# Small transfers of a recurrence loop on ScalarE's hardware DMA queue instead of GpSimd's software queue

## The chip, the cores and the metric

One core of one Trainium2 chip. The metric is the device time of one execution in microseconds, lower is better. Engines are named as in the profile: PE (matmul), PEld (its weight load), DVE (VectorE), ACT (ScalarE), POOL (GpSimd), SP (SyncE); a `q` behind a name is that engine's instruction queue, which issues DMA transfers. L658 is a line of the kernel's source.

## The reference, cut to what matters

There are two independent parts. Part A is a long convolution and is the first 440 us of the kernel; the change does not touch it. Part B is a recurrence over 64 segments of 32 tokens with 8 tokens of memory:

```python
mem = mem0                                              # [1, 8, 1024]
for s in range(64):
    h = concat([mem, x[:, 32*s:32*s+32]], axis=1)       # 40 tokens
    q, k, v = (einsum('btd,dhe->bhte', h, W) for W in (Wq, Wk, Wv))   # 32 heads of 128
    o = attention(q, k, v)                              # memory tokens are seen by all
    o = einsum('bhte,hed->btd', o, Wo)
    mem = o[:, :8]                                      # goes into the next step
    outs.append(o[:, 8:])                               # 32 tokens to the output
```

Every step needs all four weight matrices (64 chunks of 512 KB), and step s+1 can't start before `mem` of step s is there.

## The kernel before

Most weight chunks stay in SBUF. Those that don't fit, 19 in each step, are streamed from a scratch tensor `WS` into a ring of six slots by SP. A chunk is fetched as soon as PE has used up the one whose slot it takes:

```python
RING = 6
def slot():
    k = free.pop(0)
    t = ring.tile([128, 2048], BF, tag=f"wring{k}", name="wring")
    return k, t
def fetch():
    if loads:
        s, ch = loads.pop(0)
        live[s, ch] = k, t = slot()
        nc.sync.dma_start(t[:], stream_src(ch))      # 512 KB
def done(ch):                                        # behind the matmuls of a streamed chunk
    free.append(live.pop((now[0], ch))[0])
    ...
    fetch()
```

The small transfers of a step, all from GpSimd, in software:

```python
def load_x(s):                        # 192 KB: the tokens and last tokens' K and Q of step s
    rec = one.tile([128, 768], BF, tag="rec", name="rec")
    nc.gpsimd.dma_start(rec[:], REC[:, s, :])
    ...
class Tail:                           # output rows of two steps together, every second step
    def store(self):
        YB = one.tile([128, 256], BF, tag="QT", name="YB")
        nc.vector.tensor_copy(YB[:], self.acc)
        for dq in range(4):           # 4 x 8 KB
            nc.gpsimd.dma_start(bass.AP(outb.tensor, ..., [[2048 * SEG, NB], [2048, 8], [1, 256]]),
                                YB[32 * dq:32 * dq + W, :])
# ... in each step s
VBs = one.tile([128, 2, 128], BF, tag="VBs", name="VBs")       # 64 KB: last tokens' V
nc.gpsimd.dma_start(VBs[:]..., VBD[s].rearrange("t c i w -> (c i) t w"))
# ... projections, attention, output projection
if not last: load_x(s + 1)            # behind the last V projection
# ...
nc.scalar.copy(Y[:], yacc[:, 0:256])
nc.gpsimd.dma_start(bass.AP(outb.tensor, outb.offset + SEG * s * 2048,
                            [[256, 4], [2048, 32], [1, 256]]), Y[:])   # 64 KB, rows of 512 bytes
```

One thing is not in the source: the build. It gives each hardware transfer, whether from SP or from ACT, one of eight completion semaphores, in turn and in the order of the program. A transfer that gets a semaphore waits at its issue until the last transfer that had it has landed. Before, the chunks of 600 to 2100 us use eight semaphore numbers, each 133 times. I call this order of hardware transfers "the row" below. Software transfers have eight semaphores of their own (before, numbers 111 to 118).

## Time and profile before

| | |
|---|---|
| median of 3 runs | 2195.88 us (2193.15 to 2203.36) |
| profiled span | 2198.0 us, granted TensorE clock 0.965 |
| first Y copy / last Y copy in the trace | 496.7 us / 2185.4 us |
| one step, mean | 26.80 us |

The prediction below shows the views that it rests on. How to read them: in the DMA view a queue's share is the time that its packets took, as a share of 16 engines' time; q1 is SP's hardware queue, q10 ACT's, q0 the software queue. In the waits of SP's queue, `SPq L658 <- X: total, times, longest` says how long the issue of a weight chunk stood still and what ended the wait last. The moved bytes of the loop, 600 to 2100 us:

```profile
DMA packets 166936, 581.58 MB, mean 388 GB/s; under 512 B 25758, under 2 KB 25758, under 8 KB 166648
```

### The profile page before, as it was taken

The page shows a single profiled execution, that of the slowest core. Times are in us where ns is not written, and L with a number is a line of the kernel's source. Part 1 is how long each engine was busy: PE and PEld are TensorE (multiplying, and loading weights), DVE is VectorE, ACT ScalarE, POOL GpSimd, SP SyncE. Part 2 cuts the span into 40 slices and gives each one's busy share as a digit, 9 for nine tenths or more (in the row PEclk, how much of TensorE's full clock was granted, in tenths as well). Part 3 has the DMA queues.
Part 4 walks back from the last instruction along what each step waited for, and adds up shares of the span by engine and source line. Part 5 has one row for each costly group of instructions (what it writes and reads, how often), then busy time and mean ns, then how long its engine had stood idle before and what let it go on. Part 6 is the DMA issues. An engine that isn't in the chain of part 4 may idle for free. (4 is left out here: it accounts for less than half of the span.)

```text
span 2198.0 us, 81500 instructions
## 1 busy us (share of the span) xinstructions
PE 1721.9 (78%) x35607; PEld 927.7 (42%) x35636; DVE 884.2 (40%) x2702; ACT 638.6 (29%) x1118; POOL 412.2 (19%) x1103
## 2 busy tenths in 40 slices
PE   4679975957777788878888888887887878888886
PEld 2233332424444444444444444444444444444444
DVE  8827853123333333333333333333333333333332
ACT  5845530112222222222222222222222222222222
POOL 5004331001111112111111111111111211211111
PEclk9889997879999999999999999999999999999999
DMA  9989989899999999999999999999999999999997
GB/s 322 345 291 342 318 238 325 275 346 390 386 380 378 381 374 390 385 378 395 391 392 395 391 393 393 392 397 365 396 392 387 394 390 376 388 392 388 390 385 273
DMA packets 294286, 807.80 MB, mean 368 GB/s; under 512 B 84940, under 2 KB 84972, under 8 KB 293927
## 3 DMA queue, kind: packets, MB, share of 16 engines
q1 hardware_dynamic: 263592, 738.36, 89.0%
q0 software_dynamic: 23536, 50.51, 6.8%
q10 hardware_dynamic: 6800, 13.72, 1.7%
q8 instruction: 279, 4.57, 0.9%
q14 instruction: 79, 0.65, 0.1%
HBM read 743.06 MB, written 62.39 MB: 366 GB/s over the span
## 5 line engine op out<-in xcount | busy, mean ns | idle before, releaser
L806 PEld LDWEIGHTS <-rec 128*32 128x32 bf16 x12351 | 324.2, 96 | 471.6 <-issue 255.0
L806 PE MATMUL acc<-wring,rec 128*32 128x512 bf16 (+1 forms) x3777 | 374.7, 385 | 136.0 <-DMA wring<-WS 122.1
L815 ACT CAST qkv_sb<-acc 128x512 bf16<-128x512 f32 x384 | 224.8, 585 | 676.2 <-PE acc L806 645.7
L806 PE MATMUL acc<-Wres,rec 128*32 128x512 bf16 x4864 | 394.9, 383 | 1.5 <-issue 1.4
L892 PEld LDWEIGHTS <-OT 128*32 128x32 bf16 x8192 | 217.8, 96 | 178.1 <-issue 151.6
L892 PE MATMUL yacc<-Wlate,OT 128*32 128x256 bf16 x5120 | 221.8, 274 | 13.0 <-issue 11.9
L892 PE MATMUL yacc<-wring,OT 128*32 128x256 bf16 x3072 | 153.9, 276 | 98.5 <-DMA wring<-WS 59.0
L806 PE MATMUL acc<-Wmid,rec 128*32 128x512 bf16 x3072 | 226.1, 383 | 0.5 <-issue 0.5
L752 PEld LDWEIGHTS <-OTB 128*16 128x16 bf16 x4096 | 104.5, 89 | 103.9 <-issue 94.0
L878 ACT CAST OT<-OTp 128x512 bf16<-128x512 f32 x128 | 74.9, 585 | 241.4 <-PE OTp L870 241.3
L707 POOL DMA_DIRECT2D rec<-REC x64 | 37.4, 584 | 566.6 <-issue 268.9
L908 DVE COPY KT<-tps 128x512 bf16<-128x512 bf16 x64 | 27.2, 424 | 289.1 <-PE tps L821 289.1
L879 DVE CAST OTB<-OTp 128x128 bf16<-128x128 f32 x128 | 37.3, 291 | 258.6 <-ACT OT L878 258.6
L647 DVE TENSOR_SCALAR wring<-OTp 128x384 int32<-128x384 int32 x126 | 112.2, 890 | 61.5 <-PE acc L806 54.2
L752 PE MATMUL SB<-Wlate,OTB 128*16 128x256 bf16 x2480 | 98.0, 277 | 35.4 <-DVE SB L743 19.3
L782 POOL COPY KT<-rec 128x128 bf16<-128x128 bf16 x128 | 38.6, 302 | 439.2 <-PE SB L830 430.9
L836 DVE TENSOR_REDUCE mx<-SB 128x5 f32<-128x200 f32 x128 | 47.1, 368 | 182.8 <-PE SB L830 182.8
L767 POOL DMA_DIRECT2D out_dram<-YB x128 | 73.1, 578 | 236.4 <-DVE YB L765 212.9
L752 PE MATMUL SB<-wring,OTB 128*16 128x256 bf16 x1488 | 78.8, 274 | 36.5 <-DVE SB L731 30.8
L821 PE MATMUL tps<-ident,qkv_sb 128*128 128x128 bf16 x1024 | 101.2, 221 | 7.8 <-DVE wring L647 0.2
L821 PEld LDWEIGHTS <-qkv_sb 128*128 128x128 bf16 x1024 | 62.7, 97 | 104.7 <-ACT qkv_sb L815 64.4
L556 PE MATMUL kb_ps<-XBT,pw 128*128 128x512 bf16 x314 | 87.7, 400 | 9.3 <-ACT XBT L512 7.6
(214 smaller groups left out, 2300.8 us busy)
## 6 DMA issues: line engine op xcount, KB each, us to landing
wring<-WS SPq DMA_DIRECT2D x1218, 512.0 KB, 7.3
rec<-REC POOLq DMA_DIRECT2D x64, 192.0 KB, 6.0
SK<-s_sb SPq DMA_DIRECT2D x16, 512.0 KB, 4.8
SU<-s_sb SPq DMA_DIRECT2D x16, 512.0 KB, 4.6
Ug<-SU SPq DMA_DIRECT2D x32, 256.0 KB, 6.1
Kg<-SK ACTq DMA_DIRECT2D x32, 256.0 KB, 5.5
REC<-stage SPq DMA_DIRECT2D x4, 2048.0 KB, 15.2
SZ<-zs SPq DMA_DIRECT2D x31, 256.0 KB, 3.0
```

Of the source, the lines that this page charges most:

```text
L556: nc.tensor.matmul(ps[:], lhsT=ws[kc][:, hl * 128:(hl + 1) * 128], rhs=XBT[:, kc].rearrange("p s t -> p (s t)"), start=(kc == 0), stop=(kc ...
L647: nc.vector.tensor_scalar(out=dst, in0=src, scalar1=0, scalar2=None, op0=ALU.bitwise_or)
L707: nc.gpsimd.dma_start(rec[:], REC[:, s, :])
L752: nc.tensor.matmul(self.acc[32 * dq:32 * dq + W, x - o:y - o], lhsT=self.OTB[:, c, 4 * g + i, :], rhs=r, start=first and not self.seeded, ...
L767: nc.gpsimd.dma_start(bass.AP(outb.tensor, outb.offset + (SEG * NB * self.b + NX) * 2048 + 256 * dq, [[2048 * SEG, NB], [2048, 8], [1, 256 ...
L782: nc.gpsimd.tensor_copy(KT[:, :, :, 32:40], KBs[:, 128 * g:128 * g + 128].rearrange("p (c i t) -> p i c t", c=4, i=4))
L806: nc.tensor.matmul(self.acc[32 * c:32 * c + 32, x - 512 * c:y - 512 * c], lhsT=hT[:, kc, :], rhs=r, start=(kc == 0 and x == 512 * c), stop ...
L815: nc.scalar.copy(sb[:], self.acc[:])
L821: nc.tensor.transpose(tp[:, i * 128:(i + 1) * 128], sb[:, i * 128:(i + 1) * 128], ident[:])
L836: nc.vector.tensor_reduce(out=mx[:], in_=S, op=ALU.max, axis=AX.X)
L878: nc.scalar.copy(OT[:], o_view[:, :, :, 0:32])
L892: nc.tensor.matmul(yacc[32 * dq:32 * dq + 32, x - o:y - o], lhsT=OT[:, c, i, :], rhs=r, start=(h == 0 and x == o), stop=(h == 31), tile_po ...
```

## The change

The intent: in the kernel before, GpSimd's software queue costs 0.55 to 0.7 us of GpSimd for each issue and shows the first data packet some 4 us after it (3.8 us for the YB stores, median of 600 to 2100 us); I expected ACT's hardware queue to be quicker. The core of the diff (in its other lines YB's copy and YB's stores become two methods, `copy()` and `store()`, so that the stores follow the Y store):

```diff
     def load_x(s):
         rec = one.tile([128, 768], BF, tag="rec", name="rec")
-        nc.gpsimd.dma_start(rec[:], REC[:, s, :])
+        (nc.gpsimd if s == 0 else nc.scalar).dma_start(rec[:], REC[:, s, :])
@@ Tail.store
                 for dq in range(4):
-                    nc.gpsimd.dma_start(
+                    nc.scalar.dma_start(
@@ each step
-            nc.gpsimd.dma_start(VBs[:].rearrange("p g e -> p (g e)"), VBD[s].rearrange("t c i w -> (c i) t w"))
+            nc.scalar.dma_start(VBs[:].rearrange("p g e -> p (g e)"), VBD[s].rearrange("t c i w -> (c i) t w"))
@@
+            V1 = pv1.evac()
             if not last:
                 load_x(s + 1)
-            V1 = pv1.evac()
@@
-            nc.gpsimd.dma_start(bass.AP(outb.tensor, outb.offset + SEG * s * 2048, [[256, 4], [2048, 32], [1, 256]]), Y[:])
+            nc.scalar.dma_start(bass.AP(outb.tensor, outb.offset + SEG * s * 2048, [[256, 4], [2048, 32], [1, 256]]), Y[:])
             if tail is not None and not last:
                 tail.run(TURN[1])
+            if finished is not None:
+                finished.store()
```

More of the change, by code (lines that the diff above doesn't have):

```diff
@@ L741, in __init__ @@
                 self.seeded = acc is None
+                self.YB = None
                 self.left = list(range(32))
@@ L756, in head @@
                 if not self.left:
-                    self.store()
+                    self.copy()
             def run(self, n):
@@ L761, in run, with copy @@
                     self.head(h, pieces((3, h // 2, 0)))
+            def copy(self):
+                self.YB = one.tile([128, 256], BF, tag="QT", name="YB")
+                nc.vector.tensor_copy(self.YB[:], self.acc)
             def store(self):
-                YB = one.tile([128, 256], BF, tag="QT", name="YB")
-                nc.vector.tensor_copy(YB[:], self.acc)
+                YB, self.YB = self.YB, None
+                if YB is None:
+                    return
                 for dq in range(4):
-                    nc.gpsimd.dma_start(
+                    nc.scalar.dma_start(
                         bass.AP(outb.tensor, outb.offset + (SEG * NB * self.b + NX) * 2048 + 256 * dq,
@@ L948, in b_kernel @@
             nc.scalar.copy(Y[:], yacc[:, 0:256])
+            finished = tail
             if j == NB - 1 and not last:
@@ L954, in b_kernel @@
                 fill_mem(pend[s + 1][0], Y)
-            nc.gpsimd.dma_start(bass.AP(outb.tensor, outb.offset + SEG * s * 2048, [[256, 4], [2048, 32], [1, 256]]), Y[:])
+            nc.scalar.dma_start(bass.AP(outb.tensor, outb.offset + SEG * s * 2048, [[256, 4], [2048, 32], [1, 256]]), Y[:])
             if tail is not None and not last:
                 tail.run(TURN[1])
+            if finished is not None:
+                finished.store()
             if last:
                 own.run(32)
+                own.store()
 @with_exitstack
```

## The prediction

The sum came to +97 us over 2195.9: 81 for the 31 steps with YB stores, 21 for the 33 others (0.65 us each, "engine load"), and about -5 for the end; that made 2293, and less 8 for rival 2 it is the 2285. The 21 us rested on which DMA engines take a store's rows from step to step, and the records, which do not name the engine of a packet, don't show that. The sum of rival 3 and the ground for the 2330 of rival 4 rested on the same.

> **What bounds the kernel now.** I read first the busy strip of the page, then the chain of work that ended last, then the DMA view of the middle of the loop, then the waits of SP's queue, and last the timeline of one step's end.
>
> The strip has one digit (tenths busy) for each of 40 slices of 55 us:
>
> ```profile
> PE   4679975957777788878888888887887878888886
> ...
> DMA  9989989899999999999999999999999999999997
> ```
>
> From slice 9 on (the recurrence, 64 steps from about 460 us to the end) PE is 80% busy and the 16 DMA engines are never free. The chain, followed back through the last 380 us or so, agrees: of the 17% of the span that it covers, 11 are weight chunks on their way into the ring.
>
> ```profile
> DMA 11%; PE 3%; DVE 2%; issue 1%; ACT 0%; POOL 0%; SPq 0%; DVEq 0%; POOLq 0%; ACTq 0%
> ```
>
> The DMA view of 600 to 2100 us (queue: packets, MB, share of the engines' time; then issues with KB and us to landing) holds 56 steps, so a step is 1500/56 = 26.8 us:
>
> ```profile
> q1 hardware_dynamic: 153208, 557.89, 96.2%
> q0 software_dynamic: 13440, 19.42, 3.9%
> ...
> wring<-WS SPq DMA_DIRECT2D x1064, 512.0 KB, 7.2
> rec<-REC POOLq DMA_DIRECT2D x56, 192.0 KB, 6.1
> out_dram<-Y POOLq DMA_DIRECT2D x56, 64.0 KB, 6.4
> VBs<-VBD POOLq DMA_DIRECT2D x56, 64.0 KB, 6.3
> out_dram<-YB POOLq DMA_DIRECT2D x112, 8.0 KB, 5.0
> ```
>
> A step has 19 chunks of 512 KB (1064/56), one each 1.35 us; all the small transfers together take 3.9%, 1.04 us. A chunk lands 7.2 us after its issue, so 7.2/1.35 = 5.3 of the six ring slots are on their way: the queue is full, and this depth is what keeps the engines busy. What makes SP wait (us in total, times, longest):
>
> ```profile
> SPq L658 <- PE acc L806: 461.1, 681, 3.7
> ...
> SPq L658 <- DMA wring<-WS: 282.4, 559, 2.0
> ```
>
> SP issues a chunk as soon as a slot is free. So only two things can move the time: what the busiest DMA engine has to do in a step, and whether SP can keep the queue filled.
>
> [...] in 440 to 480 us the hardware queue of ACT,
>
> ```profile
> q10 hardware_dynamic: 1568, 3.16, 23.2%
> ```
>
> holds in the packet records 1440 data packets and 128 completions: 16 for each of six weight loads and 8 for each of the four loads of 8 rows. [...] In the records, packets of the record load do stand alternately with chunk packets. [...] the YB stores issued at 1381.46 us show their first data packet at 1385.4.
>
> **The change part by part.**
>
> Issue cost. GpSimd loses 0.55 to 0.7 us for each of its transfers; it is not in the chain, so nothing comes of it but at the end. ACT gains them. Its old hardware issues took about 0.33 us (256 KB loads). One step's end:
>
> ```profile
> 1380.96 0.37 ACT L948 CAST Y<-yacc 128x256 bf16<-128x256 f32 x1 [3.39 <-PE yacc L892]
> ...
> 1381.46 2.29 POOL L767 DMA_DIRECT2D out_dram<-YB  x4 [6.59 <-DVE YB L765]
> ...
> 1383.74 0.69 POOL L955 DMA_DIRECT2D out_dram<-Y  x1
> ...
> 1384.42 0.55 POOL L778 DMA_DIRECT2D VBs<-VBD  x1
> ...
> 1386.70 0.58 ACT L815 CAST qkv_sb<-acc 128x512 bf16<-128x512 f32 x1 [5.37 <-PE acc L806]
> ```
>
> ACT is idle for 5.4 us just there; six issues of 0.33 are 2 us. The record load after the V evacuation falls into another gap. Cost on the path: 0.
>
> Engine load. In the records a software packet joins descriptors to 4096 bytes (159 to 170 ns, as a chunk's packet), but a hardware packet is one row. A 512-byte row: between 464 and 467 us ten rows and ten completions,
>
> ```profile
> q10 hardware_dynamic: 20, 0.01, 0.8%
> ```
>
> are 0.8% of 48 engine-us, 0.38 us; less ten completions of 9 ns, 29 ns a row. (The records say 27.) [...]
>
> Queue depth, the part that I hold to be the largest. The build gives every hardware transfer one of eight completion semaphores in turn, and a transfer waits for the last user of its own. In the kernel before only chunks stand in that row, and 8 back is never behind the six slots. Now Y, four YB and VBs stand in it too. The listing of SP's instructions with their waits, at the end of a step with YB stores (the wait after the comma is the slot's own):
>
> ```
> 544 L658 DMACopy wring_13350<-WS_59 128x2048 [waits DMAHW7_49,DMAHW2_49,PE_49]
> 545 L658 DMACopy wring_13378<-WS_59 128x2048 [waits DMAHW4_49,DMAHW0_49,PE_49]
> 546 L658 DMACopy wring_13446<-WS_59 128x2048 [waits DMAHW5_49,DMAHW1_49,PE_49]
> ```
>
> HW4 is the Y store's, HW5 the first YB store's. So chunk 13378 can't be issued before Y has landed, and SP keeps order, so nor can any later one. In the trace before it was issued at 1380.73, before Y was even copied. Worked out on those times: the chunks on their way at 1380.7 (issued at 1374.84, 1376.34, 1379.74, and the next, held until about 1382) last for 4 x 1.35 = 5.4 us, to about 1386.1. Y is issued at 1381.4 and starts at about 1383 (my estimate); to 1386.1 16 of its 32 rows pass, each in turn with a chunk packet (27 + 162 ns); the rest need 16 x 27 = 0.4 us and the landing some 0.5: Y lands at about 1387, the next chunk's data come 1.7 us later (estimate), 1388.7. The engines stand for 1388.7 - 1386.1 = 2.6 us. YB's rows and half of Y's pass in that hole, so the engine load of such a step is mostly inside it. A step without YB has three semaphores fewer in the way: there Y's is due seven chunks on, when Y has landed or nearly so; no hole.
>
> Sum: 31 steps with YB x 2.6 = 81; [...] the end of the kernel, where GpSimd's eight stores of 0.57 us stand in the chain, about -4 or -5. Together +97, so about 2293; I take some of it back for rival 2: **2285 us**.
>
> **The rivals.**
> 1. Nothing but the issuer changes: the DMA time is the same, and the software queue's 4 us to the first packet were hidden. For it: small transfers are 3.9%. Against it: the waits above, which are in the program. It would make 2190 to 2200.
> 2. The software queue disturbs the chunks, and its going helps. In the records a chunk packet within 0.2 us of a software packet takes 175.8 ns on average, one far from any 164.9; that is up to 0.35 us a step, 22 us in all. Alone it would make about 2170; with the rest it softens the rise.
> 3. Only the engine load counts, the semaphore waits are met early[...].
> 4. QT0 waits for the landing of YB (same buffer). [...] Then 2330 or more.
>
> **Range and chances.** Rival 3 and a hole of 1.5 us set the low side, 2215; rival 4 or a hole of 4 us the high side, 2350. Within 2% ends at 2240: that needs the hole to be nearly absent or the engine load to be spread. Slower by over 2% 0.86, within 0.12, faster by over 2% 0.02.
>
> **What would show it.** Right: in the waits of SP's queue, new rows of chunks waiting for out_dram<-Y or <-YB with one to several us each in some 31 steps; the strip of DMA falls below 9 in slices, and GB/s of the loop from 388 to about 368; the share of a software queue in the loop is 0, q10 has 128 + 128 + 128 row packets a step and more; steps with YB longer than the others by 2 us. Wrong: the DMA share stays at 100% with the time up (engine load or slower packets, not depth), or ACT waits for DMA ahead of an evacuation that PE needs, or the time stays and the waits for Y are short because a hardware store lands much sooner than I estimate.

What the traces show beside its figures:

- Engines. In the packet records a hardware transfer sends 16 completion packets, or fewer; I take one as one engine's. After, in 600 to 2100 us, the counts fit 16 for the record, 16 for VBs, 4 for Y and 2 for each YB store (53 x 36 + 26 x 8 = 2116, all there are). So Y is 32 rows on each of four engines.
- Packets. Before, software packets have 4096 bytes (median 165 ns, the middle half 159 to 174), those of the record 4608 and 3072; a chunk's packets have 4096 (median 162 ns, 159 to 165). After, a row of 512 bytes is one packet, median 27 ns.
- Alternation. Before, the last two packets of the record load issued at 1374.30 start 0.342 us apart, which is the 180 ns of the first and one chunk packet (162). After, the last rows of Y in the step of 1394.8 pass 0.18 us apart.
- Its estimates of 1.6 us from Y's issue to its first row, 0.5 to the landing and 1.7 from a chunk's issue to its data give no source. Before, the ACT load issued at 128.72, after 116 us without a packet on its queue, took 1.56 us to its first packet; after, Y took 1.77 in the step shown below (medians 1.6 in steps with YB stores, 3.6 in the others), its semaphore was full 0.40 us after the last completion packet, and the data of the chunk issued at 1427.25 began 1.0 us later.

## The result, and the profile after

| | before | after |
|---|---|---|
| median of 4 runs each, same chip | 2197.89 us (2193.15 to 2203.36) | 2287.23 us (2279.73 to 2291.67) |
| ratio | | 1.0402, 95% interval 1.0362 to 1.0442 |
| profiled span, granted clock | 2198.0 us, 0.965 | 2288.1 us, 0.953 |

A ratio here and below is the mean time of one kernel's fast runs over the mean of the other's in the same rounds, so it is not quite the ratio of the medians. Differences in us are differences of medians of the same rounds.

Where the 90 us are. In the trace, the first Y copy is at 496.4 us (before 496.7), so nothing changed ahead of the loop. The last Y copy is at 2277.4 us (2185.4): 63 steps of 28.27 us instead of 26.80, +92.3 us. From there to the end it takes 10.64 us (12.60), -2.0 us. Counted from Y copy to Y copy, the 30 steps that begin with YB stores take 28.90 us (before 26.88), the 33 without take 27.70 (26.73).

The chain that ended last, by engine, has more DMA than before (14 for 11%):

```profile
DMA 14%; PE 4%; DVE 1%; issue 1%; ACT 0%; ACTq 0%; SPq 0%; POOL 0%; DVEq 0%; POOLq 0%
```

The DMA view of the loop, 600 to 2100 us, as before. No line of the software queue is left:

```profile
DMA packets 169645, 551.14 MB, mean 367 GB/s; under 512 B 18253, under 2 KB 40269, under 8 KB 169371
...
q1 hardware_dynamic: 145239, 528.87, 91.5%
q10 hardware_dynamic: 24132, 18.23, 3.7%
```

The engines are not busier, they are less busy: 91.5 + 3.7% instead of 96.2 + 3.9%. So what was added is not work, it is standing still. The waits of SP's queue, whole execution, name it (columns: us in total, times, longest):

```profile
SPq L658 <- PE acc L812: 344.7, 590, 3.2
SPq L658 <- DMA wring<-WS: 334.5, 490, 3.7
SPq L658 <- DMA out_dram<-Y: 208.5, 61, 7.8
...
SPq L658 <- DMA rec<-REC: 102.8, 32, 4.3
```

The last two rows do not exist before. A weight chunk does not use the output rows of Y or the record; it waits for them because it got their semaphore, eight transfers later. One end of a step with YB stores, timeline (start, us, engine, what; in brackets the idle time before and what ended it):

```profile
1421.11 9.12 SPq L658 DMA_DIRECT2D wring<-WS  x8
...
1422.38 0.37 ACT L954 CAST Y<-yacc 128x256 bf16<-128x256 f32 x1 [3.44 <-PE yacc L898]
...
1422.78 0.62 ACTq L962 DMA_DIRECT2D out_dram<-Y  x1
...
1423.50 2.64 ACTq L773 DMA_DIRECT2D out_dram<-YB  x4
...
1426.18 0.59 ACTq L784 DMA_DIRECT2D VBs<-VBD  x1
...
1427.00 0.58 ACT L821 CAST qkv_sb<-acc 128x512 bf16<-128x512 f32 x1 [4.25 <-PE acc L812]
...
1428.55 0.40 PE L812 MATMUL acc<-wring,rec 128*32 128x512 bf16 x4 [0.95 <-DMA wring<-WS]
```

The eight chunks of the first line are, by the single issue records:

```
SP issues of chunks: 1421.11  1424.01  -- 1427.25  1427.68  1428.19  1428.67  1429.14  1429.84
```

Y is issued at 1422.78, its first rows pass at 1424.55, the last of its four engines sends its completion packet at 1426.78, and its semaphore is full at 1427.18; at 1427.25 the next chunk goes, and five more that were due follow closely. SP's waits in 1418 to 1432 us hold two stops of this kind:

```profile
SPq L658 <- DMA out_dram<-Y: 2.9, 1, 2.9
SPq L658 <- DMA wring<-WS: 2.5, 1, 2.5
```

The second line is the gap before 1424.01, and it too comes from the row. Five of the seven transfers ahead of it in the row are Y and YB stores, so eight places back stands a chunk that was issued a short time ago: the one of 1424.01 had to wait until the third chunk before it, which had its semaphore, landed at 1423.95. By the semaphores' records chunks wait in this way for chunks 26 times in 600 to 2100 us, 67.3 us in all, at most 3.7; in the kernel before never.

What this does to the DMA engines stands in the table by stretches (last two columns: DMA share, GB/s). After:

```profile
1424.40:1426.40 2.00, 1.91 (x40) 0.89 (x29) 0.00 (x0) 0.00 (x0) 0.00 (x0) 1.00 0.87 299
1426.40:1428.40 2.00, 1.07 (x19) 0.45 (x16) 0.00 (x0) 0.58 (x1) 0.00 (x0) 1.00 0.55 184
1428.40:1430.40 2.00, 1.49 (x20) 0.65 (x20) 0.42 (x1) 0.00 (x0) 0.00 (x0) 1.00 1.00 338
```

Before, the same stretch counted from the Y copy, for a step of the same kind:

```profile
1385.00:1387.00 2.00, 1.75 (x32) 0.81 (x29) 0.00 (x0) 0.30 (x1) 0.84 (x5) 1.00 0.99 359
```

The engines' share falls to 0.55 for 2 us: that is the hole. In a step without YB stores there is one too, later and flatter (a share of 0.76 in 1404 to 1406 us, in the step of the next lines). Waits of SP's queue in 1394 to 1406 us:

```profile
SPq L658 <- DMA out_dram<-Y: 4.9, 1, 4.9
SPq L658 <- DMA rec<-REC: 2.8, 1, 2.8
```

There Y is issued at 1394.8 into a full queue, its first row passes at 1398.9 and it lands at 1403.9, 9.1 us after its issue. That is a long one: by the semaphores' records Y lands 7.0 us after its issue in such steps and 3.9 in steps with YB stores (medians of 600 to 2100 us).

### The profile page after: what moved, and what is told of

It reads as the page before. It is cut to its first block, busy times and chain, and to the rows that moved or that the text cites. A ratio compares the mean times of both kernels' runs of the same rounds, so it can differ in the third digit from the quotient of the medians.

```text
span 2288.1 us, 81558 instructions
## 1 busy us (share of the span) xinstructions
PE 1745.9 (76%) x35607; PEld 937.5 (41%) x35636; DVE 882.9 (39%) x2702; ACT 638.5 (28%) x1118; POOL 224.5 (10%) x784
## 5 line engine op out<-in xcount | busy, mean ns | idle before, releaser
L812 PE MATMUL acc<-wring,rec 128*32 128x512 bf16 (+1 forms) x3777 | 381.5, 392 | 204.6 <-DMA wring<-WS 191.8
L812 PE MATMUL acc<-Wres,rec 128*32 128x512 bf16 x4864 | 401.0, 389 | 0.5 <-issue 0.4
L898 PEld LDWEIGHTS <-OT 128*32 128x32 bf16 x8192 | 222.6, 98 | 179.4 <-issue 154.3
L954 ACT CAST Y<-yacc 128x256 bf16<-128x256 f32 x64 | 23.8, 372 | 247.3 <-PE yacc L898 196.8
L795 POOL COPY QBm<-rec 128x32 bf16<-128x32 bf16 x512 | 84.3, 209 | 0.0
```

Of the source, the lines that this page charges most:

```text
L795: nc.gpsimd.tensor_copy(q[:, :, 40 * i:40 * i + 8], QBs[:, 128 * g:128 * g + 128].rearrange("p (c i t) -> p c i t", c=4, i=4)[:, :, i, :])
L812: nc.tensor.matmul(self.acc[32 * c:32 * c + 32, x - 512 * c:y - 512 * c], lhsT=hT[:, kc, :], rhs=r, start=(kc == 0 and x == 512 * c), stop ...
L898: nc.tensor.matmul(yacc[32 * dq:32 * dq + 32, x - o:y - o], lhsT=OT[:, c, i, :], rhs=r, start=(h == 0 and x == o), stop=(h == 31), tile_po ...
```

## The experiments

Three theories had to be told apart. T1: SP is held at its semaphores until small transfers land, and the weight stream runs dry. T2: the small transfers cost more DMA time in hardware (rows of 512 bytes as packets of their own; by the completion packets four engines for Y and two for a YB store). T2's figures in the texts below are estimates from the row time of the records: 32 rows of 27 ns on each of Y's four engines are 0.86 us a step, 0.65 above an even spread over sixteen (128 x 27 / 16 = 0.22 us), which is 41 us in 64 steps; the four YB stores, 32 rows on each of two engines in every second step, are 0.43 us a step. They take it that the same engines get the rows in every step, which is not shown. T3, the rival of the intent: the hardware queue itself helps or does not matter. All runs but one (told there) gave correct results.

### Undoing parts of the change (e1, e2, e3)

```diff
# e1: only the Y store back to software            # e2: only the YB stores back to software
-            nc.scalar.dma_start(<Y store>)        -                    nc.scalar.dma_start(<YB store>)
+            nc.gpsimd.dma_start(<Y store>)        +                    nc.gpsimd.dma_start(<YB store>)
# e3: both
```

> The changed kernel (2287 us) with the Y store alone back on GpSimd's software queue. Theory 1 (a chunk is held at SP until the small store that last used its completion semaphore has landed, and the queue runs dry): the rows of SP waiting for out_dram<-Y (208 us) go, YB stores no longer stand behind Y's 32 rows and land early, so most of the 91 us comes back: 2205 to 2225. Theory 2 [...]: Y's 0.65 us a step go, YB's 0.43 stay: about 2245.

> The changed kernel with the YB stores alone back on the software queue. Theory 1: the hole at the end of every second step becomes the smaller one of the other steps, but Y is still waited for in every step: 2245 to 2260. Theory 2: only YB's 0.43 us a step go: about 2260. Steps with YB become as long as the others under both.

> The changed kernel with Y and YB stores both on the software queue; records and VBs stay on ACT's hardware queue, where they use all 16 engines. Theories 1 and 2: nothing of the 91 us is left, 2190 to 2205. If the hardware queue's one-row packets or ACT's issue time were the cause, 15 us or more would be left.

| | median us | over before (2195.39) | ratio |
|---|---|---|---|
| e1 | 2258.02 | +62.6 | 1.0272 (1.0225 to 1.0319) |
| e2 | 2240.52 | +45.1 | 1.0217 (1.0165 to 1.0269) |
| e3 | 2229.23 | +33.8 | 1.0162 (1.0112 to 1.0212) |

My numbers were missed in e1 and e3, and e2 fell a little below them (its steps with YB stores do become about as long as the others, 27.57 and 27.90 us). I had thought of one transfer as the culprit, with the rest harmless; e3 has only the record load and VBs in hardware, both spread over all 16 engines (16 completions each: 15840 packets of ACT's queue for 110 transfers of 128 rows), and a third of the loss is still there. For that case I had written down one-row packets or ACT's issue time as the cause; e10 below, where the record load goes the same way at no cost, speaks against both. SP's waits in its loop (600 to 2100 us) say why:

```profile
SPq L658 <- DMA rec<-REC: 191.1, 54, 5.0
...
SPq L658 <- DMA VBs<-VBD: 55.4, 33, 3.0
```

Taking some transfers out of the row shifts the rest in it. In the changed kernel a chunk waited for the record in 27 of these steps (86.5 us), here in 54. So parts undone one by one do not add up, and these three runs can't separate T1 from T2.

### The Y store over 16 engines (e4)

```diff
+    YSC = dram.tile([n_seg, 128, 512], BF, name="YSC")
-            nc.scalar.dma_start(<Y store to the output, 4 x 32 rows>)
+            nc.scalar.dma_start(YSC[s, :, 0:256], Y[:])
```

The rows go to a scratch tensor with the 128 partitions outermost, so the output is wrong. That Y uses 16 engines then is carried over from the record load and VBs, which have 128 rows outermost and 16 completions; Y's own completions were not counted here, nor those of e6 and e8 below.

> The changed kernel, wrong on purpose: Y goes to a scratch tensor whose slowest dimension is 128, so that all 16 engines share its rows; the same bytes, rows, queue and completion semaphores. Theory 2: -0.65 us a step, about 2245, and the waits for Y may stay. Theory 1: Y lands with 8 rows an engine instead of 32, some 4 us sooner, so most of the waits for Y go as well: about 2220.

It took 2265.36 us (ratio 1.0321, 1.0285 to 1.0357), 70.0 over before, where the changed kernel was 89.3 over in its own rounds: some 20 us less, and less gain than either theory had. SP waits for Y 140.1 us in 52 waits, 2.7 each, while the record's wait (87.3 us in 26) stays. All of the gain is in the steps without YB stores: they fall from 27.70 to 26.84 us, and there Y lands 5.7 us after its issue in place of 7.0 (medians); steps with YB stores take 29.14. The gain can be read as load or as landing time, so the next four runs separate these.

### One added store, on 4 or 16 engines, in the middle or at the end of a step (e5 to e8)

The kernel before, plus one 64 KB store a step from ACT's hardware queue, of a constant tile to scratch. Bytes and rows are the same in all four. In e5 and e7 a store has four completions (e7: 7392 packets of ACT's queue for 56 stores, 128 + 4 each).

```diff
+    YSC = dram.tile([n_seg, 32, 2048], BF, name="YSC")
# e5, e6: behind the evacuation of V0; e7, e8: behind the Y store
+            if s > 0:
+                nc.scalar.dma_start(bass.AP(YSC.tensor, YSC.offset + 32 * 2048 * s, AP), WB[:, 0:256])
# AP of e5, e7 (4 engines):  [[256, 4], [2048, 32], [1, 256]]
# AP of e6, e8 (16 engines): [[512, 128], [1, 256]]
```

> The kernel before (2197 us) with one more hardware store a step from ACT, 64 KB of a constant tile to a scratch tensor with Y's shape (4 x 32 rows of 512 bytes, four engines), issued in the middle of the step, where the chunk that next uses its completion semaphore is due some 10 us later. Theory 2: [...] +50 to +55: about 2250. Theory 1: no hole, only 0.22 us a step of more bytes: about 2210.

> The same store in the middle of the step with 128 as its slowest dimension, on 16 engines. Both theories: +14 (64 x 0.22 us of more bytes): about 2210. The difference to the four-engine store is the engine load by itself: 41 us under theory 2, 0 under theory 1.

> The same four-engine store, issued at the end of the step behind the Y store, where three of the eight chunks that follow it in the program have been issued before it runs. Theory 1: the chunk that reuses its semaphore is held until it has landed (about 9 us after its issue), a hole of about 0.5 us a step: 20 to 40 us more than the same store in the middle of the step. Theory 2: as in the middle of the step, within 5 us.

> The 16-engine store at the end of the step: it lands about 5 us after its issue, so the chunk that reuses its semaphore is hardly held. Both theories: about 2210, as in the middle of the step, within 5 us.

| | place, engines | median us | over before (2194.87) | ratio |
|---|---|---|---|---|
| e5 | middle, 4 | 2315.59 | +120.7 | 1.0558 (1.0531 to 1.0585) |
| e6 | middle, 16 | 2205.76 | +10.9 | 1.0044 (1.0014 to 1.0073) |
| e7 | end, 4 | 2215.36 | +20.5 | 1.0099 (1.0078 to 1.0120) |
| e8 | end, 16 | 2200.83 | +6.0 | 1.0023 (1.0006 to 1.0041) |

The misses taught most: the same 32 rows on each of four engines cost 15 us over sixteen at the end of a step (e7 less e8), and 110 us in the middle (e5 less e6). Load on four engines is the same in both places. So if it costs as much in the one as in the other, load by itself is about 15 us at most, 0.23 us a step; no run shows apart from the wait what it costs in the middle. I had the places the wrong way round. SP's waits in the loop, e5 and then e7:

```profile
SPq L659 <- DMA YSC<-WB: 244.1, 51, 7.2
```

```profile
SPq L659 <- DMA YSC<-WB: 133.2, 50, 5.9
```

In e5 a wait is 4.8 us long on average, in e7 2.7. In one step of e5 the store was issued at 1425.1 us, showed its first row at 1428.9 and landed by 1434.7, 9.7 us after its issue. The first row comes no sooner in e7: 3.9 us after the issue in both (medians of 600 to 2100 us). But from the first row to the last it takes 5.7 us in e5 and 2.4 in e7, and the chunks move at 358 GB/s meanwhile in e5, at 283 in e7: as I read it, the rows take turns with chunk packets (as the last rows of Y do after, 0.18 us apart for a row of 27 ns), and in e7 fewer of those are there. So the store lands 9.8 us after its issue in e5 and 6.2 in e7; on sixteen engines, which would be 8 rows on each in place of 32, it lands after 5.8 us in e6. So few engines do matter here, by a later landing (9.8 us for 5.8). And in e5 the chunk that has its semaphore falls at the step's end, where SP refills five or six slots almost back to back.

### The same transfers, with the waits moved off SP (e9, e10)

This pair is the direct test. The record load and the Y store go through ACT's hardware queue; VBs and YB stay in software. Three tiny hardware stores (16 rows of 32 bytes) are added in each step, so that a step has exactly 24 hardware transfers (19 + 2 + 3) and each keeps its semaphore. In e10 the tiny stores stand eight behind the Y store and eight behind the record load; then ACT's tiny stores wait for the small transfers, and no chunk does. (They hardly have to: none of ACT's 283 issues in 600 to 2100 us stands for 0.1 us.) In e9 they stand elsewhere.

```diff
+    FIL = dram.tile([n_seg, 3, 16, 16], BF, name="FIL")
+    def filler(*fs):
+        if 0 < now[0] < n_seg - 1:
+            for f in fs:
+                nc.scalar.dma_start(FIL[now[0], f], WB[0:16, 0:16])
     def fetch():
+        if count[0] == 8:        # e9: 4          (fetches so far in this step)
+            filler(0)
+        # e9 alone: if count[0] == 16: filler(1, 2)
+        count[0] += 1
@@
             nc.scalar.copy(Y[:], yacc[:, 0:256])
+            filler(1, 2)         # e10 alone
```

The program's order of hardware transfers in one step of e10, with the number of the semaphore, shows the pattern (`c` is a chunk, F a tiny store): `c1 Y2 c3 c4 c5 c6 c7 c0 c1 F2 c3 c4 c5 c6 c7 rec0 c1 c2 c3 c4 c5 c6 F7 F0`. Semaphore 2 of Y goes to F2, semaphore 0 of the record to F0.

> The kernel before with the record load and the Y store alone on ScalarE's hardware queue (last tokens' V and YB stay in software), and three tiny hardware stores (16 rows of 32 bytes) a step from ScalarE, placed so that the transfer eight behind the record load and the Y store in the row of completion semaphores is still a weight chunk of SP. T1 (SP is held by the landing of a small transfer): the chunks wait, 2222 to 2245, with rows of SP waiting for rec and for out_dram<-Y of 60 us and more in the middle of the loop. T2 (rows on few engines, packets of one row, the hardware queue itself): 2210 to 2225 and the same in the next run.

> The same transfers on the same queues as in the run before this, but the three tiny stores stand eight behind the Y store and eight behind the record load, so that ScalarE's tiny stores and not SP's chunks wait for the landing of the small transfers. T1: at most 2212, 20 us or more below the run before this, and no rows of SP waiting for rec or out_dram<-Y; what is left over the kernel before is engine load and the cost of the tiny stores. T2: within 5 us of the run before this.

e9 took 2338.62 us (ratio to the 2196.39 of before 1.0623, 1.0555 to 1.0690), worse than I had for either theory and worse than the whole change. e10 took 2191.42 us (ratio 0.9977, 0.9930 to 1.0024), the same as before. The same transfers on the same queue with the same rows and engines: 147 us apart, by which instruction has to wait for their semaphores. SP's waits in the loop of e9:

```profile
SPq L671 <- DMA out_dram<-Y: 239.1, 46, 8.0
SPq L671 <- DMA rec<-REC: 221.7, 52, 5.4
```

In the loop of e10 these rows are gone, and chunks wait for tiny stores, shortly:

```profile
SPq L669 <- DMA FIL<-WB: 203.3, 134, 3.5
```

1.5 us each, and harmless: the loop of e10 moves 390 GB/s (e9 356, before 388). T1 holds, and for Y and the record load T2 has nothing left to explain: Y runs on four engines in rows of 512 bytes in e10 too (the 21005 packets of ACT's queue in its loop are, but for 23 at the window's ends, 144 for each record load, 132 for each Y store and 32 for each tiny one). T3 as well: the hardware queue brings no gain that these runs can see. YB and VBs are in software in both runs; that the same holds for them is carried over, not shown.

### A wait without the hardware queue (e11, e12)

The kernel before, all small transfers in software, plus one tiny software store of 4 KB a step. In e11 it reads the ring slot that is refilled next, so SP must wait for its landing; in e12 it reads a constant tile.

```diff
+    FIL = dram.tile([n_seg, 16, 128], BF, name="FIL")
             nc.gpsimd.dma_start(<Y store>)
+            if 0 < s < n_seg - 1:
+                nc.gpsimd.dma_start(FIL[s], live[s + 1, order_s[0]][1][0:16, 0:128])   # e12: WB[0:16, 0:128]
```

> The kernel before (all small transfers in software) with one more tiny software store a step, behind the Y store, of 16 rows of 256 bytes that it reads from the ring slot whose refill is due next. SP must hold that refill until the tiny store has landed, some 5 us after its issue; no hardware queue, no row on few engines. T1: 2250 to 2330, with a row of SP waiting for the tiny store of 3 to 6 us in each step. T2: 2195 to 2205, since 4 KB a step is nothing.

> The control of the run before this: the same tiny software store in the same place, but read from a tile that no transfer writes, so that nothing waits for it. Both theories: 2195 to 2205.

e11 took 2394.15 us (ratio 1.0885, 1.0837 to 1.0934), beyond the range I gave; e12 2199.88 us (1.0010, 0.9967 to 1.0053). One held chunk a step, with no hardware transfer beside the chunks, costs 198 us. (GpSimd itself is not held: the tiny store is issued as soon as Y's issue ends, and lands 4.9 us after its own, median.)

```profile
SPq L659 <- DMA FIL<-wring: 351.0, 50, 8.4
```

That is 7.0 us each, where I had expected 3 to 6.

### What a hold costs

From the waits of SP's queue in 600 to 2100 us (total over times) and the mean step of the whole loop (before 26.80 us):

| kernel | mean wait of a chunk for a small transfer, us | step, us over before |
|---|---|---|
| e6 | 1.2 (39 times) | +0.09 |
| e10 | 1.5 (134 times) | -0.11 |
| e8 | 1.7 (48) | -0.01 |
| e7 | 2.7 (50) | +0.31 |
| e3 | rec 3.5 (54), VBs 1.7 (33) | +0.49 |
| e2 | Y 3.6 (50), rec 3.3 (28), VBs 0.8 (39) | +0.94 |
| e1 | rec 3.4 (27), VBs 1.7 (31), YB 1.2 (33) | +1.09 |
| e4 | Y 2.7 (52), rec 3.4 (26), VBs 0.9 (14) | +1.13 |
| after | Y 3.3 (51), rec 3.2 (27) | +1.46 |
| e5 | 4.8 (51) | +1.84 |
| e9 | Y 5.2 (46), rec 4.3 (52) | +2.33 |
| e11 | 7.0 (50) | +3.14 |

Waits of 1.2 to 1.7 us (e6, e10, e8) were all but free, -0.11 to +0.09 us a step. As I read it, the 5.3 chunks on their way (7.2 us to landing, one each 1.35) bridge them, and the ring refills. With waits of 2.7 us and more (e7 and the rows below it) the step grew by 0.31 us and more, so a part of the longer waits was lost. How large a part is not settled. e1 waits less for small transfers than e3 and loses twice as much, and the changed kernel loses more than e3 and e5 suggest. What the table leaves out are the waits of chunks for chunks that the filled row makes: 98.0 us in e1, 67.3 after, 70.4 in e4, 63.7 in e9, and none in e2, e3 and e5 to e8 (in e10 48.6 us, 0.7 each). With these counted, what the waits exceed 2 us by comes to 0.9 us a step in e7, 1.2 in e1, 1.6 in e3, 2.3 in e2 and in the changed kernel, and from a third to nine tenths of it is lost. No run takes the two kinds one by one.

No version beat the kernel before: e10 is equal to it within its interval.

## Why the prediction was right or wrong, point by point

- **Time, direction, bandwidth.** 2285 predicted, 2287.23 measured; 368 GB/s in the loop predicted, 367 measured. The mechanism, SP held by the semaphores of small transfers, is shown by e9 against e10 and by e11 against e12. But that the sum came so near is luck, of errors that cancelled: the steps with YB cost 60 us (30 x 2.0) for 81, the others 32 (33 x 0.97) for 21, the end gave 2 for 4.5, and the 8 us taken back for rival 2 were not there.
- **"Issue cost".** ACT's issues of row-wise stores took 0.59 to 0.64 us (medians of Y, YB and VBs), not 0.33; only the record's took 0.33. Six in a row are 3.9 us in the step shown, in place of 2. It was off the path there: ACT's next evacuation waited for PE until 1427.00, 0.2 us after the last issue. In 7 of the 26 such steps in 600 to 2100 us the evacuation starts within 0.07 us of the last issue's end, so ACT is the later one; in the two that were looked at PE next stands for a chunk (0.77 and 0.84 us), and nothing is lost by it.
- **"Engine load", +0.65 us a step (21 us of the sum).** It was the author's estimate, and the term was wrong. e7 less e8 leaves about 0.23 us a step for the same rows, and part of that is a longer wait; e10, with Y on four engines, is 5 us below before, with zero inside its interval. What few engines do is to make the store land later (9.8 us after its issue in e5, 5.8 in e6, as far as e6 uses sixteen).
- **"Queue depth", a hole of 2.6 us in steps with YB.** Right in kind and nearly in size: such steps grew by 2.0 us, the engines' share fell to 0.55. Y landed 4.4 us after its copy (1426.78 against 1422.38; 4.8 by its semaphore), where I had 6 (1387 against 1380.96). The chunk "held until about 1382", 1.0 us after the copy, came too: it went at 1424.01, 1.6 after it. I misread the listing for it, without effect: in its first line the wait ahead of the comma is the slot's, and the one behind it that of the chunk's own semaphore (in the trace 108 and 103, and it uses 103).
- **"A step without YB ... no hole".** Wrong. Such steps grew by 0.97 us. I took it that Y would have landed when its semaphore came up again; but it is issued into a full queue, in the step shown lands 9.1 us after its issue, and holds SP for 4.9 us. Nor had I looked at the record load's place in the row, for which I had put 0.02 us of load alone: its landing held SP for 102.8 us in all. These waits took the place of the 21 us of engine load.
- **The end, -4 or -5 us.** It was -2.0 us (10.64 in place of 12.60 from the last Y copy on).
- **Rival 1** (nothing but the issuer changes, 2190 to 2200) is what happens to the record load and Y once the waits are off SP: e10, 2191.42.
- **Rival 2** (software packets disturb the chunks). No gain from their going is seen: in the records of the changed kernel a chunk packet within 0.2 us of one of ACT's packets takes 173.6 ns, any other 167.7. Before it is 175.8 and 166.2 (the prediction has 164.9, which the records don't give). So ACT's packets go with a smaller delay, 6 ns for 10, but the mean of all chunk packets is 169.0 ns, before 168.3.
- **Rival 3** (only the engine load counts) falls with e10, as far as Y goes.
- **Rival 4** (QT0 waits for YB) did not come: the last packet of ACT's queue at that step's end, those of YB and VBs included, passed at 1428.4 us, QT0 was copied at 1432.66, and in the view of the tile QT no wait for YB stands.
- **The signs.** The rows of chunks waiting for Y came, and in nearly every step (51 waits for 53 stores in 600 to 2100 us), not in every second one. The strip of DMA did not fall below 9 in the slices of the loop: a hole of 2 us is lost in a slice of 57. Steps with YB are longer than the others by 1.2 us (before 0.15), not by 2. ACT did not stand at semaphores ahead of an evacuation: none of its issues in 600 to 2100 us stands for 0.4 us.

## What to carry to other kernels

Here a weight stream that was kept full by depth (5.3 chunks on their way) stood still for the landing of newcomers that shared its eight completion semaphores: 208.5 us for Y and 102.8 for the record in the changed kernel, which was 4.0% slower. So before a transfer is moved onto a queue of such a build, look in the program for what stands eight (or whatever the count) behind it. A transfer's landing, not its bytes, was what counted (e5 and e6, the same bytes, are 110 us apart), and under the full stream the median landing came 6 to 10 us after the issue (by semaphore: 6.7 for the record, 7.3 for Y in e10, 10.2 for the store of e5). The newcomers also took semaphores from the stream: in the changed kernel chunks waited for chunks 26 times, 67.3 us in all, before never. If the move is wanted all the same, put an instruction that can afford the wait at the place where the semaphore comes round: so done in e10, the move of the record load and Y was even (0.9977).
